# First batch: the coarse 1/sum moves from a GpSimd product into the matmul that transposes

## The chip, the cores and the metric

One core of a Trainium2 chip runs the whole program. The metric is the device time of one execution in microseconds (us). The kernel before takes 667.07 us, the median of three runs (666.96 to 668.61). A core has TensorE (PE, matmuls), VectorE (DVE), ScalarE (ACT), GpSimd (POOL) and SyncE (SP, which issues the loads and stores here), each with its own instruction list that it works through in order.

## The reference, cut to what matters

Three layers in a row, on 4 batches of 576 positions. The first is an attention of 8 heads of 64, the sum of two parts:

```python
q_d = q.reshape(B, H, Sd, 4, D).mean(axis=3)       # k_d, v_d likewise: 144 positions
out_d = sm_attn(q_d, k_d, v_d)                     # softmax(q k^T / 8) v, coarse
out_up = np.repeat(out_d, 4, axis=2)
mask = np.abs(pos[:, None] - pos[None, :]) < 4     # local: 7 neighbours
out = out_up + softmax(masked scores) @ v
```

The second adds the real part of a Fourier transform over positions and features, normalises, and applies two weight matrices of 512x2048 and 2048x512 with a ReLU between them. The third is a gated convolution with two weights of 512x512. Of all this the change touches the softmax of the coarse attention: exp(s) divided by its sum, times v.

## The kernel before, in words

**Stages.** The attention and the Fourier step of batch 0 are written out in `chain0`; those of batches 1 to 3 in `attn_steps`. The two later layers run in 12 units of 192 positions; the attention of a later batch is worked in between the units of an earlier one. Batch 0 has nothing to be worked in between, except the preparation of the weights: they come as 64-bit words, and three integer operations on VectorE (`word_op`, lines 547 and, through the helper `stt`, 448) rebuild each block of 128x1024 as 32-bit floats. The first layer's matmuls (line 1160, in f32 for the first positions, and 1196 with two halves in f16) need the centred result u (line 1711) of batch 0.

**The coarse attention of batch 0.** Four items a = 0 to 3, of two heads each (`par`). For each item: `coarse` puts the scores of 144x144 into PSUM as two halves of 72 rows (line 1518); `coarse_max` takes the row maxima on VectorE; `coarse_exp` makes exp on ScalarE into the tile E with the row sums beside it (line 1534); `coarse_norm` adds 1e-9 to the sums, takes the reciprocal (lines 1539, 1540) and multiplies E by it on GpSimd, one product of 72x288 per head (through the helper `mul`, so its line is 451):

```python
for par in range(2):
    mul(G, E[:, par], E[:, par], s_[:, par].unsqueeze(2).to_broadcast([QC, 2, SD]))
```

`coarse_turn` transposes E in four pieces of 72x72 per head on TensorE, with E as the stationary operand and the identity `eye` as the moving one (line 1549), and ScalarE evicts the result as ET (line 1552); `coarse_value` multiplies it by v (line 1558) into `base`.

**Beside it** runs the local attention of batch 0 in three groups: scores (line 1439), maxima, exp on ScalarE in pieces of 64 columns (line 1462), normalisation on VectorE (`score_norm`), transposes (line 1476), values (line 1495), and the sum with `base` into X on VectorE (`value_add`). The Fourier step follows.

**In batches 1 to 3** the coarse attention is in `lowres`; there the normalisation is either GpSimd's product (`if b in EN_G`, which holds batch 1 alone) or two ScalarE products of 72x144 per head (line 906).

**Order of the work.** Each step of the program has a number, in the order in which the steps are written into the program. The table `ORDER` gives for each engine its whole instruction list in these numbers ("48.1" is the second instruction of step 48 on that engine). Steps that the text names: 48, 54, 71, 85 are the normalisations of the items a = 0 to 3; 75, 68, 73 are three weight operations; 2, 4, 7, 9 the loads of the parts of q (7 and 9 the second parts, 9 for items 2 and 3), 1, 3, 6, 8 those of k; 11, 13, 14 those of v0, v1, v2; 16.1 a table of 512 KB for the Fourier step. `CHAIN0` gives the order in which batch 0's steps are written. Before the first loads arrive, TensorE runs filler matmuls on the tile `busy` (`fill`, line 1418), which GpSimd has set to 1.

Of the kernel before, what the change touches and what calls it, by code (L numbers as in the profile page):

```python
# [9 lines left out]
F32 = mybir.dt.float32  # L10
# [9 lines left out]
SD = S // 4  # L20
# [60 lines left out]
263.1 296.2 291.2 302 296.1 291.3 394.0 265.0 288.3 265.2 298.3 265.1 288.0 263.3 265.3 306 315 267.0-1 319 269.0-1  # L81
295.0 267.2 269.2 296.0 301 327 272.0 288.1 272.1 274.0 288.4 274.1 288.5 298.2 275.0 288.2 275.1 311 298.0-1 289.3
277.0-1 289.0 277.2 289.1 289.4-5 289.2 277.3 278 394.1 283.0-1 318.0-1 283.2 334 330 283.3-4 286.0 291.4 286.1-2
342.0 314 342.1 318.2 283.5 303.0 305.0 283.6 290.2 290.1 320.1 346 320.3 290.0 318.3 321.1 321.3 303.1 320.0 320.2
323.1 305.1 349 321.0 331 325.0 324 356 321.2 323.3 323.0 323.2 325.1 326.3 326.1-2 326.0 333 394.2 363 339.0 336.0
339.1-2 336.1 325.2-3 347.0 347.3 347.2 337.1 337.0 339.3 348.3 348.2 348.0 351.0 370 394.3 351.2 347.1 339.4 348.1
339.5-7 358 351.3 337.2-3 378 384 353.2-3 339.8-9 368.3 394.4 351.1 368.0 353.0-1 339.10 388 316 368.1 368.4 368.2
368.5 369.0 372.3 396 372.0 364.0 369.1 374.0 393.0 364.1 372.1-2 372.4-5 393.1 400.1 402.1 376.0 374.1 376.3 383.2-3
405 399 376.1 406.1 376.2 376.4-5 380.3 380.0 400.0 400.3 416 413 380.1 402.0 380.2 380.4-5 374.2-3 426 374.4 383.0
406.0 390.0 383.1 387.0-1 418 391.0 429 387.2 390.1 391.2 390.2 391.1 390.3 387.3 391.3 390.4 395.1 395.0 390.5-6  # L90
398.0-1 395.2 390.7 398.2 390.8 522.0 432 390.9 400.2 404 446.1 374.5 435 402.3 402.2 410.1 406.2-3 374.6 390.10 408
439 407 446.0 410.0 410.3 441 410.2 411.0 411.2 411.1 443 522.1 411.3 430.0 414 457 423.0 436.0-1 423.1 428.1 428.0
430.1 449 446.2 436.2-3 422 436.4 428.2 455 428.3 436.5 434.1 444.1 436.6 434.0 444.3 436.7 425 447.1 458 444.0 444.2
462 436.8 447.0 447.3 447.2 450.3 450.2 450.1 522.2 453.3 450.0 453.2 453.1 436.9-11 434.2-3 453.0 451.1 451.0 463.0
460.0 436.12-13 466 468 460.1 522.4 436.14 451.2-3 473 463.1 478 483.0 486.3 486.0 489 480 481.0 486.4 486.1 486.5
481.3 481.2 488.3 427 492.3 492.0 486.2 483.1-2 504 483.3 492.1 499 483.4 488.2 492.4 492.2 492.5 495.0 503 483.5-8
488.0 490.3 497.3 497.0 495.1 509 506.2 483.9 522.3 497.4-5 497.1-2 495.2 490.0 490.2 481.1 502.3 502.0 495.3 488.1
# [1833 lines left out]
```

## Time and profile before

| | |
|---|---|
| median of the runs | 667.07 us |
| profiled execution, its own time | 668.18 us |
| its span, first to last instruction | 666.4 us |
| TensorE busy | 647.4 us (97%) |
| VectorE busy | 458.3 us (69%) |
| ScalarE busy | 328.5 us (49%) |
| GpSimd busy | 127.1 us (19%) |
| mean granted clock of TensorE | 0.985 of 2.4 GHz |

The profile is that of one execution. The busy times are sums over stages that have different limits; which engine a stage waits for is read from its timeline and its waits. A granted clock of 0.50 is 1.2 GHz. In the rows, `out<-in` are the tiles written and read, `x8` counts records, and what stands in brackets is the idle time of that engine just before, with what ended it.

### The profile page before, as it was taken

What the parts mean: (1) busy time and instruction counts of PE and PEld (TensorE: products, weight loads), DVE (VectorE), ACT (ScalarE), POOL (GpSimd) and SP (SyncE); (2) the same over time, 40 slices, a digit from 0 to 9 for tenths busy, and PEclk for the clock granted to TensorE, in tenths of its full rate; (3) what the DMA queues carried; (4) which work ended last, traced back from release to release, by engine and by line L of the source; (5) the groups of instructions that cost most, each with busy time, mean ns of one, the idle gap of its engine ahead of it and who ended that gap; (6) DMA issues with size and microseconds to landing.
All of it is one profiled execution on the core that took longest, in us unless ns stands there. A gap on an engine that the chain in (4) does not pass through costs nothing.

```text
span 666.4 us, 18165 instructions
## 1 busy us (share of the span) xinstructions
PE 647.4 (97%) x7751; PEld 581.6 (87%) x7751; DVE 458.3 (69%) x950; ACT 328.5 (49%) x997; POOL 127.1 (19%) x178
## 2 busy tenths in 40 slices
PE   8968999999999999999999999999999999999997
PEld 4647799999998887989988898998999989999895
DVE  3679999989998877657876645675447763562344
ACT  3665577888334757675235576643232313312122
POOL 0240306321210613501110352030001020000000
PEclk9959999999999999999999999999999999999999
DMA  8976072313424001403240020000300000000001
GB/s 301 402 247 243 2 253 82 101 34 100 161 60 171 20 18 46 142 1 104 77 150 2 27 62 17 3 1 25 116 2 17 2 1 33 1 2 18 2 32 48
DMA packets 23299, 52.08 MB, mean 78 GB/s; under 512 B 1855, under 2 KB 11071, under 8 KB 22194
## 3 DMA queue, kind: packets, MB, share of 16 engines
q1 hardware_dynamic: 23218, 50.91, 22.4%
q8 instruction: 61, 1.00, 0.6%
q14 instruction: 20, 0.16, 0.1%
HBM read 44.41 MB, written 8.26 MB: 79 GB/s over the span
## 4 chain that ended last, share of the span: by engine, by line
PE 78%; DVE 11%; issue 5%; DMA 3%; POOL 2%; ACT 1%; SPq 0%; POOLq 0%; ACTq 0%
PE ph L1196 25%; PE pc L1216 24%; PE out L1324 7%; PE val L1308 7%; DVE W L448 5%; PE ab L996 2%; POOL E L451 1%; PE dO L805 1%; PE po L1572 1%; PE st L1080 1%; PE sc L883 1%; DMA raw<-in_moe_w_ch_dram 1%; PE pc L1171 1%; DMA kTa<-in_k_dram 1%; PE dPT L788 1%
## 5 line engine op out<-in xcount | busy, mean ns | idle before, releaser
L1196 PE MATMUL ph<-uh,W 128*128 128x192 f16 x1408 | 198.3, 246 | 1.3 <-DVE hl L448 0.7
L1196 PEld LDWEIGHTS <-W 128*128 128x128 f16 x2112 | 176.8, 98 | 9.5 <-issue 4.3
L1216 PE MATMUL pc<-hh,W 128*128 128x192 f16 x1232 | 171.7, 246 | 0.0
L1196 PE MATMUL ph<-ul,W 128*128 128x192 f16 x704 | 171.2, 246 | 0.0
L1216 PEld LDWEIGHTS <-W 128*128 128x128 f16 x1848 | 154.3, 98 | 5.7 <-issue 1.4
L1216 PE MATMUL pc<-hl,W 128*128 128x192 f16 x616 | 129.5, 246 | 0.0
L1200 ACT ACTIVATE hh<-ph 128x384 f16<-128x384 f32 x88 | 42.7, 488 | 125.8 <-PE ph L1196 100.5
L448 DVE SCALAR_TENSOR_TENSOR hl<-ph,hh 128x384 f16<-128x384 f32 x88 | 48.2, 552 | 77.6 <-ACT hh L1200 77.4
L448 DVE SCALAR_TENSOR_TENSOR W<-X,cw,W 128x192 f32<-128x192 f32 x160 | 64.1, 437 | 2.7 <-ACT W L1271 2.3
L1308 PE MATMUL val<-yy,W 128*128 128x192 f16 x576 | 59.6, 246 | 0.5 <-ACT yy L1250 0.5
L1308 PEld LDWEIGHTS <-W 128*128 128x128 f16 x576 | 48.5, 98 | 1.1 <-issue 0.4
L1324 PE MATMUL out<-W,gh 128*128 128x512 f16 x144 | 46.5, 379 | 0.0
L769 ACT ACTIVATE dP<-dS,dmx 128x64 f32<-128x64 f32 x120 | 36.2, 329 | 0.6 <-PE dPT L788 0.3
L448 DVE SCALAR_TENSOR_TENSOR W<-W,W 128x1024 int32<-128x1024 int32 x24 | 29.5, 1237 | 0.1
L451 POOL TENSOR_TENSOR E<-E,lsu 72x288 f32<-72x288 f32 x16 | 18.9, 1197 | 55.1 <-ACT nm L1529 19.7
L454 POOL TENSOR_TENSOR sq<-sq 128x384 f32<-128x384 f32 (+1 forms) x12 | 10.6, 880 | 93.6 <-ACT sq L1091 93.2
L1324 PE MATMUL out<-W,gl 128*128 128x512 f16 x72 | 27.1, 379 | 0.0
L769 ACT ACTIVATION_READ_ACCUMULATOR dP<-dS,dmx 128x1 f32 x120 | 26.7, 223 | 0.0
L1324 PEld LDWEIGHTS <-gh 128*128 128x128 f16 x144 | 14.0, 98 | 12.0 <-issue 0.2
L1216 PE MATMUL pc<-hh,Wz 128*128 128x192 f16 x176 | 24.3, 246 | 0.0
L1171 PE MATMUL pc<-h,W 128*128 128x192 f32 x128 | 23.3, 329 | 0.0
L1160 PE MATMUL ph<-u,W 128*128 128x192 f32 x128 | 22.5, 327 | 0.4 <-DVE u L1711 0.4
(288 smaller groups left out, 1212.0 us busy)
## 6 DMA issues: line engine op xcount, KB each, us to landing
W<-in_moe_w_ch_dram SPq DMA_DIRECT2D x12, 1024.0 KB
out_dram<-osb SPq DMA_DIRECT2D x17, 256.0 KB
vw<-in_vw_dram SPq DMA_DIRECT2D x8, 512.0 KB
v<-in_vp_dram SPq DMA_DIRECT2D x24, 144.0 KB
X<-in_q_dram SPq DMA_DIRECT2D x6, 576.0 KB
kT<-in_k_dram SPq DMA_DIRECT2D x4, 582.0 KB
X<-in_moe_w_ch_dram SPq DMA_DIRECT2D x2, 1024.0 KB
raw<-in_moe_w_ch_dram SPq DMA_DIRECT2D x4, 512.0 KB
```

What stands on the lines that cost most here:

```text
L448: return eng.scalar_tensor_tensor(out=out, in0=in0, scalar=scalar, in1=in1, op0=op0, op1=op1)
L451: return eng.tensor_tensor(out=out, in0=a, in1=b, op=ALU.mult)
L454: return eng.tensor_tensor(out=out, in0=a, in1=b, op=ALU.add)
L769: A.activation(out=s_[:, z, a], in_=pss[par][:, z, a], func=AF.Exp, scale=SCALE, bias=mx[:, par, z, a:a + 1], accum_out=su[:, par, z, a:a ...
L996: T.matmul(out=ps[0:n, c0:c1], lhsT=d[x][:, c, sd, e, n0:n0 + n], rhs=feat[:, w, c, c0:c1], start=(t == 0), stop=(t == 5),)
L1160: T.matmul(out=ps[:, e], lhsT=W[AT[kc * 2 + m // 8] + 1][:, o:o + 128], rhs=u()[:, kc, :], start=(kc == 0), stop=(kc == 3))
L1171: T.matmul(out=c["ps"][m // 2][:, m % 2], lhsT=W[9 + g][:, o:o + 128], rhs=hs[g // 2][:, g % 2, e, :], start=(kk == 0 and m % 2 == 0), sto ...
L1196: T.matmul(out=ps[:, e], lhsT=w1_ap(pw, kc, 2 * g + e), rhs=uh[px][:, kc, :], start=(t == 0), stop=(t == 11))
L1200: A.activation(out=h_, in_=ps, func=AF.Relu)
L1216: T.matmul(out=ps[m // 2][:, m % 2], lhsT=w2_ap(pw, kk, m), rhs=x[px][:, e, :], start=(kk == 0 and (pw, px) == (0, 0) and m % 2 == 0), sto ...
L1308: T.matmul(out=ps[:, e], lhsT=wv_ap(pw, kc, 2 * mh + e), rhs=m_["y"][px][:, kc, :], start=(t == 0), stop=(t == 11))
L1324: T.matmul(out=ps, lhsT=(gh, gl)[px][:, kc, t * 128:(t + 1) * 128], rhs=wo_ap(pw, kc), start=(n == 0), stop=(n == 11))
```

## The change

In batch 0, `coarse_norm` no longer multiplies E. VectorE makes, per head, a tile `dg` of 72 x (2 x 72) from the identity and the reciprocal sums: two diagonal matrices. `coarse_turn` then multiplies E by the diagonal matrix instead of the identity, as a plain f32 matmul in place of the transpose; the result is the transposed and scaled E. `EN_G` becomes empty, so batch 1 uses ScalarE's products like batches 2 and 3. The tile `busy` is 128 columns wide in place of 512, and the filler matmul reads it four times over. All five lists of `ORDER` are new, the tile slots are not.

```diff
-EN_G = (1,)
+EN_G = ()
...
-    busy = const.tile([P, 512], F16, name="busy")
+    busy = const.tile([P, P], F16, name="busy")
...
-                    T.matmul(out=ps, lhsT=busy[:, 0:P], rhs=busy, start=True, stop=True)
+                    T.matmul(out=ps.rearrange("p (a c) -> p a c", c=P), lhsT=busy, rhs=busy.unsqueeze(1).to_broadcast([P, 4, P]), start=True, stop=True)
...
             V.reciprocal(out=s_, in_=s_)
             for par in range(2):
-                mul(G, E[:, par], E[:, par], s_[:, par].unsqueeze(2).to_broadcast([QC, 2, SD]))
+                lr["dg", a, par] = sp.tile([QC, 2, QC], F32, tag="dg", name="dg", bufs=3)
+                mul(V, lr["dg", a, par], eye[0:QC, 0:QC].unsqueeze(1).to_broadcast([QC, 2, QC]),
+                    s_[:, par].unsqueeze(2).to_broadcast([QC, 2, QC]))
...
-                        T.transpose(out=pe[:, kc, qc], in_=lr["E", a][:, par, qc, kc * QC:(kc + 1) * QC],
-                                    identity=eye[0:QC, 0:QC])
+                        T.matmul(out=pe[:, kc, qc], lhsT=lr["E", a][:, par, qc, kc * QC:(kc + 1) * QC],
+                                 rhs=lr["dg", a, par][:, qc], start=True, stop=True)
```

Of the new lists, the starts that bear on batch 0 (SyncE's, GpSimd's and VectorE's):

```diff
-0 2 1 4 7 3 5.0 11 5.1 6 13 9 8 14 10 15.2 12 15.1 16.0 15.3-4 195.1 16.1 15.0 119.2 15.5 119.3 185.0 123.1 16.2 119.0
+0 2 1 4 3 5 13 11 6 16.0 7 14 16.1 8 9 10 15.0-1 12 15.3 15.5 15.4 119.2 185.0 15.2 195 123.1 123.0 122.0 16.2 119.0
...
-0.0 5 48.1 48.0 54 71 85 136.1 136.0 137 139.1 139.0 0.1 195.1 195.0 195.2 183.0-1 183.3 183.2 193 211.1 211.0 229
+0.0 5 136 195.1 0.1 137 139.1 139.0 121 195.0 183.0-2 193.0-6 183.3 193.7-8 211.1 211.0 286.0 229.1 195.2 217.0-1
...
-21 20 30 18 25 32.0-1 32.3 32.2 41 48.0 38.1 38.0 48.1 28 23 27 58.0 54 65 58.1 0 31 71 77.1 77.0 60 34 81.0 85.0 81.1
-85.1 42 55 59 67 68 75 83 52.0 86 52.1 81.2 131.0 52.2-3 81.3 93 81.4-5 92 70.0 129 70.1 56 70.2-3 97 63 98 73 102 79
+30.0 20.1 20.0 30.1 18 21 32 25 28 41 48.0 38 48.1 23 0 131.0 48.2-3 54.0 56 27 54.1 63 31 54.3 54.2 34 58.0 131.1 42
+65 59 58.1 55 71.0 131.2 71.1-3 77 75 68 73 85 81.0 84 81.1 86 67 81.2 52.0 81.3 52.1 130 52.2-3 70.0 92 70.1 93 70.3
```

## Rows read from the trace of the kernel before

**Rows 1.** The page's busy time, share of the span and instructions, of TensorE.
```profile
PE 647.4 (97%) x7751; PEld 581.6 (87%) x7751; DVE 458.3 (69%) x950; ACT 328.5 (49%) x997; POOL 127.1 (19%) x178
```

**Rows 2.** Stretches: length, then each engine's busy us, granted clock, DMA.
```profile
9.07:79.00 69.93, 59.00 (x707) 44.36 (x707) 57.68 (x112) 43.71 (x175) 17.94 (x21) 0.85 0.70 253
10.00:30.00 20.00, 18.91 (x267) 13.22 (x267) 13.73 (x29) 13.13 (x68) 2.58 (x4) 1.00 1.02 396
30.00:50.00 20.00, 13.94 (x141) 10.07 (x143) 14.92 (x34) 13.78 (x73) 10.24 (x4) 0.54 0.80 265
31.00:32.00 1.00, 0.82 (x6) 0.38 (x5) 1.00 (x3) 0.51 (x3) 1.00 (x2) 0.84 1.00 327
41.00:52.00 11.00, 10.31 (x126) 8.18 (x127) 7.24 (x20) 7.70 (x39) 0.72 (x2) 0.50 0.44 92
50.00:79.00 29.00, 26.15 (x310) 21.07 (x306) 28.11 (x50) 16.80 (x37) 5.12 (x13) 0.96 0.39 141
140.00:170.00 30.00, 30.00 (x413) 28.34 (x410) 27.84 (x70) 23.34 (x66) 5.78 (x8) 1.00 0.24 79
```

**Rows 3.** TensorE's waits to 130 us: total, times, longest.
```profile
PE eT L1549 <- POOL E L451: 4.5, 1, 4.5
...
PE po L1418 <- POOL busy L472: 1.3, 1, 1.3
```

**Rows 4.** GpSimd's timeline: start, us, line, operation, idle before.
```profile
21.12 1.29 POOL L451 TENSOR_TENSOR E<-E,lsu 72x288 f32<-72x288 f32 x2 [19.67 <-ACT nm L1529]
...
30.94 2.94 POOL L451 TENSOR_TENSOR E<-E,lsu 72x288 f32<-72x288 f32 x2 [2.28 <-DVE lsu L1540]
34.42 7.30 POOL L451 TENSOR_TENSOR E<-E,lsu 72x288 f32<-72x288 f32 x2 [0.54 <-DVE lsu L1540]
```

**Rows 5.** Tile lsu: minimum, median, maximum ns, of whole run.
```profile
L906 ACT ACTIVATE E<-E,lsu x32: 397/402/419, 280.5 to 431.4; 72x144 f32<-72x144 f32 x32
...
L451 POOL TENSOR_TENSOR E<-E,lsu x16: 661/665/6678, 21.1 to 169.6; 72x288 f32<-72x288 f32 x16
```

**Rows 6.** TensorE's timeline, two sets of transposes.
```profile
29.04 0.67 PE L1549 MATMUL eT<-eye,E 72*72 72x72 f32 x8 [0.70 <-ACT base L1560]
...
41.15 1.32 PE L1549 MATMUL eT<-eye,E 72*72 72x72 f32 x8 [4.50 <-POOL E L451]
```

**Rows 7.** ScalarE's timeline, the eviction behind the stall.
```profile
41.88 0.41 ACT L1552 ACTIVATE ET<-eT 72x288 f32<-72x288 f32 x1 [4.58 <-PE eT L1549]
```

**Rows 8.** VectorE's waits to 130 us: total, times, longest.
```profile
DVE dsu L1467 <- ACT dP L1462: 4.2, 1, 4.2
```

**Rows 9.** TensorE's timeline, the first matmuls of the first layer.
```profile
79.00 2.87 PE L1160 MATMUL ph<-u,W 128*128 128x192 f32 x16 [0.41 <-DVE u L1711]
```

**Rows 10.** VectorE by form, 14 to 47 us: busy us, mean ns.
```profile
L448 DVE SCALAR_TENSOR_TENSOR W<-X,W 128x1024 int32<-128x1024 int32 x4 | 4.8, 1200 | 0.0
...
L547 DVE TENSOR_SCALAR W<-W 128x1024 int32<-128x1024 int32 x4 | 2.7, 683 | 0.0
...
L451 DVE TENSOR_TENSOR dP<-dP,dsu 128x256 f32<-128x256 f32 x2 | 0.8, 422 | 0.0
...
L451 DVE TENSOR_TENSOR tr<-cv,eye 128x128 f32<-128x128 f32 x1 | 0.3, 291 | 2.6 <-PE cv L1585 2.6
```

**Rows 11.** TensorE by form, to 56 us: records, busy us, mean ns.
```profile
L1549 PE MATMUL eT<-eye,E 72*72 72x72 f32 x32 | 4.5, 277 | 5.2 <-POOL E L451 4.5 <-ACT base L1560 0.7
L1476 PE MATMUL dPT<-eye,dP 128*128 128x128 f32 x20 | 4.5, 386 | 0.4 <-DVE dP L451 0.4
L1518 PE MATMUL sc<-qkT 64*72 64x144 f32 x32 | 3.6, 295 | 0.3 <-ACT E L1534 0.3
```

**Rows 12.** TensorE's waits after 130 us, first and last of four.
```profile
PE ph L1196 <- DVE hl L448: 0.7, 1, 0.7
...
PE pq L1019 <- ACT DS L1046: 0.2, 1, 0.2
```

**Rows 13.** ScalarE's waits from 130 to 200 us.
```profile
ACT hh L1200 <- PE ph L1196: 8.1, 5, 2.7
```

More of the change, by code (lines that the diff above doesn't have):

```diff
@@ L81 @@
[L81 to L85, printed above, removed]
@@ new lines @@
+216.0-1 219 197.4 173.1-2 197.5 220 188 239.4-6 250 221 189 251 231.3 231.0 217.1 222 224 247.2 231.4 247.0-1 257
+241.3 247.3 217.0 231.1 241.0 231.2 231.5 225 245.0 216.2-3 226 216.4-5 245.1 228 284.0 241.1 245.2 261 266 241.2
+241.4 245.3-4 241.5 249.3 245.5 249.0 284.1-2 233 294.0 294.2-3 245.6-8 270 245.9 291.0 245.10 249.1 245.11 249.2
+295.3 295.2 245.12 296.2 245.13 235 253.0-1 245.14 249.4-5 255.3 255.0 284.3-4 259.1 280 295.0 255.4 276 255.1-2
+253.2-3 238 294.1 253.5 284.5 253.4 243 255.5 285.0 295.1 285.1-5 259.0 292 287.1 297 263.0 265.0 287.0 263.2 263.1
@@ L141 @@
+590.2 602 605 609 595 593.1 606 612 601 614 621 619 607 610 620.1-2 620.0 632 627 623.0 634 620.3 638 635 625 623.1
+641 643 649 631 636 651 648 656 639 660 650.3 650.2 650.1 650.0 663 666 664 654 668 670 683 685 677 661 686.1 674 675
+684 688 686.0 687 689 690 691
 """,
     "tensor": """
[L143 to L144 removed]
@@ new lines @@
+324.0-3 356.14-20 363.3-8 333.17-22 324.4-7 356.21-23 363.9-20 324.8-11 370.0-3 333.23 370.4-11 335.0-3 357.22
+357.16-17 357.23 370.12-18 363.21-23 335.6 335.4-5 335.8 335.7 335.9-19 366.6 366.0 366.7 366.1 366.8 366.2 366.9
+366.3 370.19-21 336 378.0-13 366.10-11 366.4-5 339.0 366.18-20 366.12 366.21 366.13-15 366.22-23 366.16 378.14-20
+370.22 341 337.0-31 337.33 337.32 339.1 378.21-23 366.17 373.6 373.0 370.23 373.1-3 373.7-8 373.4 345 388.0-1 373.9-10
+373.5 373.11-12 373.18 373.13 373.19-22 373.14-16 373.23 373.17 381.0 381.6 381.1 381.7-8 350.4-6 350.0 350.7 381.2
@@ new lines @@
+437.20-21 437.14 437.22 437.15 437.23 438.6 408.0-21 437.16-17 408.22-23 438.0-2 438.7-10 438.3 438.11 438.4-5
+438.12-13 438.18-20 438.14-16 438.21-22 438.17 438.23 423.22-23 443.0-9 441.0-13 443.10-11 411.9 411.0-1 411.10
+411.2-3 411.11-15 411.4 411.16-17 411.5-8 441.14-23 411.18-26 443.12-15 445.6 443.16-23 449.0-3 414.0-1 445.0-1 445.7
+445.2 445.8 445.3 445.9-10 445.4-5 445.11 414.2-5 414.9 414.6 414.10-12 414.7 414.13 414.8 414.14-17 449.4-18
+445.12-14 445.18 445.15 445.19-21 445.16 445.22 445.17 445.23 455.0-1 452.0 428.1 428.0 428.2-17 455.2-21 436.0 452.1
@@ new lines @@
+452.6-8 449.19 452.2-3 452.9-10 452.4 452.11 455.22-23 449.20-23 446.0-6 462.0-13 452.5 452.18 452.12-14 452.19
+452.15-16 452.20-23 452.17 434.0 462.14 446.7 456.0 456.6-9 456.1-3 456.10-11 456.18 456.4-5 458.0-8 462.15-17
+458.9-12 446.8-11 436.1 456.12 456.19 462.18-19 458.13-16 434.1 456.13 448.0-3 458.17-20 434.2-29 448.4-12 448.14
+448.13 448.15-19 434.30-31 434.33 434.32 462.20 456.14-16 456.20-23 456.17 458.21-23 459.0-8 462.21-23 461.0 461.6
+461.1 460.0-3 459.9-11 461.2-3 461.7 461.4-5 461.12-14 461.8-9 461.15 460.4-6 468.0 463.0-1 460.7-20 468.1-7 461.10-11
@@ new lines @@
+461.16 461.18 461.17 461.19-20 466.0-5 468.8-17 461.21 460.21-23 451.0-1 461.22 466.6-10 451.2-31 451.33 451.32
+464.0-1 466.11-16 468.18 461.23 466.17-23 468.19-23 464.2 464.6 464.3 464.7-8 464.4-5 464.9 464.12 464.10 464.13
+464.11 464.18-19 464.14-15 464.20-23 464.16-17 463.2-23 478.0-6 465.0-2 465.4-7 465.3 480.0 467.6-8 467.0 467.9
+467.1-3 467.10 467.4-5 467.12 467.11 467.18-20 467.13 467.21 467.14-16 467.22 467.17 467.23 465.8-9 465.12 465.10
+465.13 465.16 465.11 465.14 465.17 465.20-21 465.15 465.18-19 465.22-26 465.28 465.27 465.29-36 465.38-39 465.37 470.0
@@ new lines @@
+594.5 594.12 594.19 594.13 593.1 597.19 602.11-19 594.20-21 594.14 606.0 602.20-23 597.20-23 594.15 594.22 594.16-17
+594.23 599.0-1 599.6-8 599.2 599.9 599.3 599.10-11 599.4-5 599.12 599.18-19 599.13-16 599.20-22 599.17 599.23 595.0-2
+603.0-1 603.6 603.2-3 603.7 603.4-5 603.12 603.8-10 603.13-16 603.11 603.18-19 603.17 603.20-21 605.0-16 606.1
+605.17-23 603.22-23 609.0-4 595.3-11 612.0 609.5-8 606.2 609.9-23 612.1-13 606.3-5 608.6-7 608.0 608.8 612.14-21
+614.0-6 607.0 608.1-2 608.9 614.7-8 608.3 608.10 608.4 608.11 608.18 608.5 614.9-17 612.22-23 608.19-21 608.12-15
@@ new lines @@
+608.22 608.16-17 608.23 606.6-7 611.6 611.0 611.7 611.1 611.8-10 611.2-3 611.11 611.18 611.4-5 606.8-11 611.12-14
+611.19-21 611.15-16 611.22 611.17 611.23 607.1 610.0-1 613.0 613.6-8 613.1 613.9-10 613.2-4 613.11 613.5 613.12 613.18
+613.13 613.19-22 613.14 607.2-9 619.0-4 614.18-23 610.2-10 613.15-17 613.23 615.0 615.6 619.5-11 621.0-7 607.10-11
+619.12-14 607.12 610.11-12 621.8-23 619.15-16 615.1 615.7-8 615.2 615.9 615.3-4 619.17 610.13-14 619.18 615.5
+615.12-13 615.10-11 615.18-22 615.14-16 615.23 615.17 619.19 616.0 616.6 616.1 616.7 616.2-3 616.8-9 616.4 616.10
@@ L296 @@
+669.11 669.14-15 669.18-21 669.16-17 669.22-23 670.18-23 671.6-8 671.0-1 671.9-10 671.2-5 671.11-12 671.18-19
+671.13-16 671.20-21 671.17 671.22-23 672.0 672.12 672.1-11 672.13-23 675.0-17 685 675.18 674.4-23 688.0-7 689.0-9
+688.8-19 675.19-23 688.20-23 689.10-23 687 690.0-5 691.0-3 690.6-11 691.4-11
 """,
```

416 lines of the change are left out of this document (195 added, 221 removed), and 7 rows, old and new, of the table ORDER.

## The prediction

> **What bounds the kernel now.** I began with the page's busy shares: TensorE is busy 97% of the 666.4 us span [rows 1], so a change can win only where TensorE stands or where its clock is low. The stretches of the span say where that is [rows 2]: from 140 to 170 us TensorE has no gap at all, at full clock, while from 30 to 50 us it is busy 13.94 of 20 us at a granted clock of 0.54. This is the first batch's attention, which nothing else can hide, since the first layer's large matmuls need its result. The list of TensorE's waits up to 130 us names one large one: 4.5 us for GpSimd's product at line 451, writing E [rows 3]. The timelines show what happens there. GpSimd does the 1/sum products in pairs; two pairs take 1.29 us, the third 2.94, and the last runs from 34.42 to 41.72, 7.30 us [rows 4]. Its longest single product takes 6,678 ns where the median is 665 [rows 5]. VectorE meanwhile runs the integer operations that rebuild the weights. TensorE stands 4.5 us until the transposes at 41.15 [rows 6]. ScalarE, in order, has the eviction of these transposes ahead of the exponentials of two local groups and stands 4.58 us; VectorE then stands 4.2 us, because its next instruction wants those exponentials [rows 7, 8]. So one late GpSimd result holds three engines for over four microseconds. After it VectorE is nearly full, 28.11 of the 29 us from 50 to 79 [rows 2], until the centred u and the first layer's first matmul at 79.00 [rows 9]. From there on TensorE's list is full, so the end should follow that instant nearly one for one.
>
> **The change part by part.** *Removed in the first batch:* eight GpSimd products (four pairs), 12.8 us of GpSimd time together [rows 4]. Only the last pair's excess is on the path. Its sums' reciprocal, the last instruction before it, was ready before 34.42.
>
> *Added on VectorE:* eight products of 72x144 that make the diagonals. None is in this trace. From below: 128x128 takes 0.291 us; from above: 128x256 takes 0.422 [rows 10]. The straight line between them gives 0.31 at 144 columns, which I take: 8 x 0.31 = 2.5 us (2.3 to 3.4). VectorE has idle time that can take it: from its first instruction at 9.07 us to 79 it is busy 57.68 of 69.93, so 12.2 us are idle, the 4.2 among them [rows 2, 8]. If none of this idle time served, the 2.5 us would all be late.
>
> *The new wait:* the last transposing matmul waits for VectorE in place of GpSimd. In VectorE's new list three weight operations (steps 75, 68, 73) stand between the last maxima and the last sums' step 85: 1.2 + 0.7 + 1.2 = 3.1 us [rows 10]. If the last sums are ready as before, at about 34.3, the two diagonals end between 34.3 + 0.6 = 34.9 and 38.0. Apart from the 4.2 us VectorE is idle only 0.9 of the 20 us there (14.92 busy, [rows 2]), so I take the late end, 38.0 against 41.72: 3.7 us earlier. Queued behind these diagonals on VectorE are the weight operations and the local normalisations, which need ScalarE's exponentials; TensorE's values step waits for those.
>
> *TensorE:* 32 transposes become 32 plain f32 matmuls. The trace has both kinds: the 16 matmuls of the coarse scores (line 1518, four for each of four items) leave 32 records, two each, while the 20 transposes of line 1476 and the 32 of line 1549 leave one each [rows 11]. A record of 72 columns is issued every (0.67 - 0.22)/7 = 0.064 us at full clock (eight records span 0.67 us, the last of them 0.22) [rows 6], so the change adds 32 x 0.064 = 2.0 us of TensorE time, and twice that at half clock. TensorE is not the limit before 36 us, so only the last item's eight are on the path: 0.5 us, or 1.0 at the half clock that stands there. I take 1.0 off the 3.7.
>
> The Trainium skill bears on this term: "TensorE: Matmul & The Clock Gate", Terms (the entry on the streaming buses), says that the transpose mode is four times faster for FP32. By it the eight last matmuls would cost three extra records each, 1.5 us at full and 3.1 at half clock, 2.1 more than I take. The trace disagrees: an f32 matmul leaves two records, not four, and a pass of an f32 matmul is issued at the pace per column of a transpose, (2.87 - 0.33)/15 = 0.169 us for 192 columns [rows 9].
>
> *After the stall:* VectorE is the nearer limit. Its idle falls by the 4.2 us; of the other 8.0 us I expect a third, 2.7, to be used, as the new list puts weight operations where it waited; it gains 2.5 us of work. That is 4.2 + 2.7 - 2.5 = 4.4 us; the bounds are 4.2 - 3.4 = 0.8 and 12.2 - 2.3 = 9.9. The path through the last diagonal gives 3.7 - 1.0 = 2.7. The two meet at the local normalisations; I take their mean, 3.5 us.
>
> *Loads:* in SyncE's new list the second parts of q and k for items 2 and 3 come behind the 512 KB of v2 and the 512 KB table, those for items 0 and 1 behind v0 and v1. At the 396 GB/s of 10 to 30 us [rows 2] a megabyte is 2.6 us. The cover is VectorE's and TensorE's other work, since these parts are wanted only at about 16 us; I charge nothing, and up to 2.6 us if the cover fails.
>
> *The second batch:* eight GpSimd products (0.665 us median, [rows 5]) become 16 ScalarE products of 402 ns, as batches three and four have them [rows 5]: 6.4 us on ScalarE between 140 and 170 us. ScalarE is busy 23.34 of these 30 us [rows 2], so 6.7 are free. I charge 0, with 0 to 6.4 as bounds.
>
> *The smaller edits:* the busy tile's memset shrinks from 0.53 us and the filler matmuls read it by a repeated pattern. TensorE's first filler waits 1.3 us for the memset [rows 3], but these fillers only pass the time until the first k and q are loaded, so nothing. The searched orders elsewhere have little to win: TensorE's four waits for other engines after 130 us, of 0.7 to 0.2 us, total 2.0 [rows 12]. Bounds -2 to +2 us; I take 0.
>
> **Sum.** The profiled execution took 668.18 us with a span of 666.4, 1.8 of it around the span. 668.18 - 3.5 = 664.7 for such an execution; it lies 1.1 above the median of the runs, 667.07, so I predict 667.07 - 3.5 = 663.6.
>
> **The rivals.**
> *A, the clock comes back too:* TensorE's 11 us from 41 to 52 run at 0.50 (1.2 GHz) [rows 2], and four idle microseconds lie before. Without them the clock may be at full for the values and transposes that follow, some 10 us of work that would take 5. VectorE's own list, bounded by 9.9, caps it. For it: the standstill goes, and 32 more records fill gaps. Against: the clock fell between 31 and 32 us (0.84) already, before the long wait [rows 2]. About 3.5 us more: 660.1. The Trainium skill leans this way ("TensorE: Matmul & The Clock Gate", Part 4: PE-mode transpose, says that transposes do not count as TensorE work for the clock as matmuls do).
>
> *B, the wait only changes its owner:* the last diagonal is late in VectorE's list, because the start is later (2.6 us of loads) or the lists in front are longer. Then it ends at about 38.0 + 2.6 = 40.6 and the gain is 41.72 - 40.6 - 1.0 = 0.1. For it: VectorE is the fullest engine there. Against: 12.2 us of idle. 667.0.
>
> *C, slower: ScalarE in the second batch.* Between 140 and 170 us it has 6.7 us free and gets 6.4. If the products stand ahead of the first layer's evictions (line 1200), TensorE, which has no gap there, waits for each. It decides when ScalarE's busy share reaches 10 of 10 while TensorE's falls under 10; price up to 6.4 us, less the 3.5 won: 670.0. Against: ScalarE's waits there are mostly for TensorE (8.1 us for line 1196 up to 200 us, [rows 13]), so it has room.
>
> **How the numbers follow.** Forecast 0.55, A 0.18, B 0.17, C 0.10. A difference under 0.3% (2.0 us) can't be told from none here. Faster than 665.1 are A and nearly all of the forecast's own range (661.5 to 665.5): 0.70. Within: B and the rest: 0.20. Slower: C: 0.10. The range from 659 to 667.5 leaves out the far part of A and C, and holds the unknown costs: 3.4 for the diagonals, 2.6 for the loads.
>
> **What would show it.** Right: no GpSimd instruction between 20 and 42 us; eight VectorE products of 72x144 at 0.3 us; 64 records for the transposing matmuls; no TensorE wait above 2 us between 30 and 50; the first matmul of line 1160 at 75 to 76 us; everything behind it earlier by as much. A shows a clock of 1.00 by 45 us. B shows TensorE waiting for VectorE's diagonal at about 38 to 41. C shows TensorE gaps between 140 and 175 us that end with ScalarE. The forecast is wrong if the first layer starts earlier and the end doesn't: then VectorE's weight work, or a load, is the limit between 80 and 200 us.

## The result, and the profile after

The changed kernel takes 661.12 us (median; 660.89 to 661.76), beside 667.84 for the kernel before on the same chip: a ratio of 0.9897, 95% interval [0.9872, 0.9922]. A second measurement gave 661.51 beside 667.03, 0.9914 [0.9900, 0.9927]. So it gains 5.5 to 6.7 us, and 663.6 was 2.5 too high. The profiled execution took 661.18 us, its span is 659.4.

One instant cuts the gain in two: the first layer's first matmul, called F below. Before, F stands at 79.00 us [rows 9] with 587.4 us of span behind it. The timeline of TensorE after has it at 73.39, with 586.0 behind it: 5.6 us are won ahead of F and 1.4 behind it. These two are the difference of two profiled executions and add up to 7.0 us, more than the medians show, because the execution before was a long one (668.18 us, beside medians of 667.0 to 667.8). Behind F three other runs with the old lists have 586.8, so 0.8 us is the safer figure there.

```profile
73.39 2.54 PE L1171 MATMUL ph<-u,W 128*128 128x192 f32 x14 [0.57 <-DVE u L1724]
```

The stretches of the kernel after, with the columns of [rows 2] (length, then busy us of TensorE, weight loads, VectorE, ScalarE, GpSimd; clock; DMA share; GB/s):

```profile
9.07:79.00 69.93, 67.18 (x786) 52.65 (x778) 65.10 (x129) 45.89 (x177) 2.57 (x13) 0.90 0.72 252
30.00:50.00 20.00, 18.19 (x232) 14.51 (x232) 19.45 (x42) 14.07 (x71) 0.00 (x0) 0.66 1.04 308
41.00:52.00 11.00, 10.22 (x187) 8.42 (x187) 10.66 (x23) 4.53 (x19) 0.00 (x0) 0.73 1.04 267
140.00:170.00 30.00, 30.00 (x413) 28.18 (x412) 27.68 (x69) 23.39 (x70) 1.21 (x1) 1.00 0.16 55
```

Read the third busy column first. VectorE is idle 69.93 - 65.10 = 4.8 us up to 79 us, where it was idle 12.2 [rows 2]; none of the 4.8 lie behind F. From 30 to 50 us it is now the fullest engine, 19.45 of 20. Its list begins with another instruction, 1.6 us later than before (the kernel before, then the kernel after):

```profile
9.07 1.35 DVE L1510 TENSOR_REDUCE qkT<-X 128x288 f32<-128x1152 f32 x1 [9.07 <-DMA X<-in_q_dram]
10.67 1.95 DVE L1463 TENSOR_REDUCE dmx<-dS 128x8 f32<-128x512 f32 x4 [10.67 <-PE dS L1450]
```

From this first instruction to F VectorE takes 62.7 us, where it took 69.9. Its wait for the exponentials, 4.2 us before [rows 8], is down to 0.4, and that for the coarse scores from 2.4 to 0.7 (the first line is the kernel before):

```profile
DVE nm L1525 <- PE sc L1518: 2.4, 3, 1.2
...
DVE nm L1536 <- PE sc L1529: 0.7, 1, 0.7
DVE dsu L1478 <- ACT dP L1473: 0.4, 1, 0.4
```

TensorE's waits up to 130 us (total, times, longest), the largest two and the one for a diagonal:

```profile
PE po L1571 <- ACT ET L1565: 1.0, 3, 0.6
PE po L1429 <- POOL mirror L492: 1.0, 1, 1.0
...
PE eT L1562 <- DVE dg L462: 0.2, 1, 0.2
```

The 4.5 us for GpSimd [rows 3] are gone and no wait of that size has come in their place. The last item's steps in VectorE's timeline, then in TensorE's:

```profile
34.40 1.21 DVE L459 SCALAR_TENSOR_TENSOR W<-X,W 128x1024 int32<-128x1024 int32 x1
35.53 0.68 DVE L558 TENSOR_SCALAR W<-W 128x1024 int32<-128x1024 int32 x1
36.13 1.22 DVE L459 SCALAR_TENSOR_TENSOR W<-W,W 128x1024 int32<-128x1024 int32 x1
37.46 0.17 DVE L1550 TENSOR_SCALAR lsu<-lsu 72x4 f32<-72x4 f32 x1
37.66 0.17 DVE L1551 RECIPROCAL lsu<-lsu 72x4 f32<-72x4 f32 x1
37.87 0.52 DVE L462 TENSOR_TENSOR dg<-eye,lsu 72x144 f32<-72x144 f32 x2
```
```profile
38.32 2.17 PE L1562 MATMUL eT<-dg,E 72*72 72x72 f32 x16 [0.18 <-DVE dg L462]
40.42 0.74 PE L1571 MATMUL po<-ET,vr 72*64 72x144 f32 x2
```

The diagonals end at 38.39, behind the three weight operations, where GpSimd's pair ended at 41.72 [rows 4]. The last item's values begin at 40.42; before, they began 2.0 us later:

```profile
42.40 1.85 PE L1558 MATMUL po<-ET,vr 72*64 72x144 f32 x8
```

The operations by form, TensorE's up to 56 us, VectorE's from 14 to 47 (count, busy us, mean ns, idle before):

```profile
L1562 PE MATMUL eT<-dg,E 72*72 72x72 f32 x64 | 7.2, 281 | 0.2 <-DVE dg L462 0.2
```
```profile
L462 DVE TENSOR_TENSOR dg<-eye,lsu 72x144 f32<-72x144 f32 x8 | 2.1, 298 | 0.1
L462 DVE TENSOR_TENSOR dP<-dP,dsu 128x256 f32<-128x256 f32 x2 | 0.8, 422 | 0.0
L462 DVE TENSOR_TENSOR tr<-cv,eye 128x128 f32<-128x128 f32 x1 | 0.3, 280 | 0.0
```

32 records have become 64, and 4.5 us of busy time 7.2 [rows 11]. A pair of diagonals takes 0.52 us, so the eight cost 2.05. The last line tells of the new order: `tr` had 2.6 us of idle before it [rows 10] and has none now.

### The profile page after: what moved, and what is told of

Read it like the earlier page. It is cut to its first block, busy times and chain, and to the rows that moved or that the text cites. A ratio compares the mean times of both kernels' runs of the same rounds, so it can differ in the third digit from the quotient of the medians.

```text
span 659.4 us, 18222 instructions
## 1 busy us (share of the span) xinstructions
PE 650.5 (99%) x7783; PEld 585.1 (89%) x7783; DVE 447.1 (68%) x958; ACT 332.6 (50%) x1013; POOL 100.6 (15%) x162
## 4 chain that ended last, share of the span: by engine, by line
PE 66%; DVE 0%; ACT 0%; POOL 0%; issue 0%; ACTq 0%
PE ph L1207 22%; PE pc L1227 22%; PE out L1335 7%; PE val L1319 7%; PE ab L1007 1%; PE st L1091 1%; PE dO L816 1%; PE po L939 1%; PE sc L894 1%; PE pp L1030 1%; PE pq L1030 1%; PE dPT L799 1%; PE eT L929 1%; PE dS L766 1%; PE pn L1030 0%; PE tps L1292 0%
## 5 line engine op out<-in xcount | busy, mean ns | idle before, releaser
L1207 PE MATMUL ph<-uh,W 128*128 128x192 f16 x1408 | 203.0, 246 | 0.5 <-ACT uh L1135 0.5
L1227 PE MATMUL pc<-hh,W 128*128 128x192 f16 x1232 | 174.6, 246 | 0.0
L459 DVE SCALAR_TENSOR_TENSOR W<-X,cw,W 128x192 f32<-128x192 f32 x160 | 61.3, 418 | 5.2 <-ACT W L1282 4.8
L1319 PE MATMUL val<-yy,W 128*128 128x192 f16 x576 | 61.0, 246 | 0.0
L1227 PEld LDWEIGHTS <-Wz 128*128 128x128 f16 x264 | 22.2, 98 | 1.7 <-DVE X L465 1.2
```

The lines of the kernel that those rows point to most:

```text
L459: return eng.scalar_tensor_tensor(out=out, in0=in0, scalar=scalar, in1=in1, op0=op0, op1=op1)
L1207: T.matmul(out=ps[:, e], lhsT=w1_ap(pw, kc, 2 * g + e), rhs=uh[px][:, kc, :], start=(t == 0), stop=(t == 11))
L1227: T.matmul(out=ps[m // 2][:, m % 2], lhsT=w2_ap(pw, kk, m), rhs=x[px][:, e, :], start=(kk == 0 and (pw, px) == (0, 0) and m % 2 == 0), sto ...
L1319: T.matmul(out=ps[:, e], lhsT=wv_ap(pw, kc, 2 * mh + e), rhs=m_["y"][px][:, kc, :], start=(t == 0), stop=(t == 11))
```

## The experiments

Every ratio is to the kernel before on the same chip.

| run | median us | ratio, 95% interval | VectorE starts, us | F, us | span, us | span less F |
|---|---|---|---|---|---|---|
| before | 667.0 to 667.8 | 1 | 9.07 | 79.00 | 666.4 | 587.4 |
| after | 661.12 | 0.9897 [0.9872, 0.9922] | 10.67 | 73.39 | 659.4 | 586.0 |
| after, again | 661.51 | 0.9914 [0.9900, 0.9927] | 10.15 | 73.00 | 659.0 | 586.0 |
| 1 old lists, diagonals | 663.90 | 0.9953 [0.9939, 0.9967] | 8.51 | 75.35 | 662.1 | 586.8 |
| 2 new lists, GpSimd products | 662.38 | 0.9937 [0.9924, 0.9950] | 10.04 | 74.58 | 660.6 | 586.0 |
| 3 old, weight words later | 668.81 | 1.0031 [1.0019, 1.0042] | 7.85 | 79.38 | 666.2 | 586.8 |
| 4 batch 1 on GpSimd, one block | 664.16 | 0.9960 [0.9947, 0.9972] | 10.33 | 73.04 | 662.4 | 589.4 |
| 5 old start of the loads | 671.46 | 1.0056 [1.0043, 1.0069] | 10.96 | 83.68 | 669.9 | 586.2 |
| 6 transposes kept | 660.70 | 0.9893 [0.9880, 0.9906] | 10.74 | 72.95 | 658.9 | 586.0 |
| 7 old, TensorE kept busy | 668.66 | 1.0017 [1.0007, 1.0026] | 8.24 | 78.77 | 665.6 | 586.8 |
| 8 diagonals made twice | 663.45 | 0.9938 [0.9926, 0.9951] | 10.95 | 75.79 | 661.8 | 586.0 |
| 9 batch 1 on GpSimd, spread | 663.93 | 0.9950 [0.9937, 0.9962] | 10.80 | 73.58 | 662.1 | 588.5 |
| 10 diagonals by ScalarE | 664.66 | 0.9961 [0.9948, 0.9974] | 10.38 | 78.01 | 664.0 | 586.0 |
| 11 old order of q and k alone | 661.25 | 0.9912 [0.9898, 0.9925] | 10.66 | 72.97 | 659.3 | 586.3 |

F moves by a few tenths from one profile to the next without any edit (73.39 and 73.00 for the same kernel), so F alone tells nothing under half a microsecond. Most of that is the start: from VectorE's first instruction to F the two take 62.72 and 62.85 us. Within one set of lists this difference is the better measure; the old lists start earlier because they begin with another instruction. Starts, F and span are those of one profiled execution, which is not always near the median: that of run 10 is the slowest of five (665.75 us), those of runs 3 and 7 are the fastest of six (667.98) and of eleven (667.42).

**1. The diagonals alone.** The kernel before, with its own lists; the eight GpSimd products become diagonals at the place of VectorE's reciprocals, and the fillers are as in the change.

```diff
-0.0 5 48.1 48.0 54 71 85 136.1 136.0 ...     (GpSimd's list)
+0.0 5 136.1 136.0 ...
-... 85.1 42 55 59 67 68 75 83 ...         (VectorE's list)
+... 85.1-3 42 55 59 67 68 75 83 ...
```

> The kernel before with its own lists and batch 1 as it was; only the diagonal (VectorE's two products stand right behind the reciprocal of each item) and the narrower busy tile. Theory (the late GpSimd product is the loss): TensorE's wait of 4.5 us at the last transposes goes, the first matmul of the first layer comes 4 to 6 us before 79.0, time 662 to 664. Rival (the new lists bring the gain): within 1 us of the kernel before, since VectorE only takes over a wait.

F comes 3.65 us earlier (3.1 from VectorE's start), somewhat less than the theory's 4 to 6, and the time falls by 3.1 us. The largest waits of TensorE up to 130 us, which say what is late next:

```profile
PE mir L1639 <- DVE X L454: 2.1, 2, 1.5
PE dPT L1476 <- DVE dP L451: 1.1, 1, 1.1
```

The stall at GpSimd is gone, and the two largest waits are now for VectorE; the first was there before (1.8 us), the second was 0.4.

**2. All but the diagonals.** The kernel after (new lists, batch 1 on ScalarE, the narrower tile), with batch 0's products put back on GpSimd and plain transposes.

```diff
+0.0 5 48 54 71 85 136 195.1 ...           (GpSimd's list)
-mul(V, lr["dg", a, par], eye ..., s_ ...)
+mul(G, E[:, par], E[:, par], s_ ...)
```

> The changed kernel with its new lists, but batch 0's products back on GpSimd and plain transposes. Theory: the last products again run beside VectorE's weight operations and take 3 us or more in place of 0.67, TensorE waits for them, time 664 to 667. Rival (new lists): 661 to 662, as the new lists put the work right whoever multiplies.

4.2 us of the gain stay without any diagonal (4.6 by the medians); the time lies between the two ranges. The diagonals are still worth something: TensorE waits 2.7 us in all for GpSimd's products, the longest 1.2, and from VectorE's first instruction to F it takes 64.5 us in place of 62.7 to 62.9. GpSimd's timeline shows why so much stays; its columns are those of [rows 4]:

```profile
21.58 1.29 POOL L462 TENSOR_TENSOR E<-E,lsu 72x288 f32<-72x288 f32 x2 [20.46 <-ACT nm L1540]
24.78 4.24 POOL L462 TENSOR_TENSOR E<-E,lsu 72x288 f32<-72x288 f32 x2 [1.92 <-DVE lsu L1551]
33.36 1.28 POOL L462 TENSOR_TENSOR E<-E,lsu 72x288 f32<-72x288 f32 x2 [4.34 <-ACT base L1571]
37.98 1.73 POOL L462 TENSOR_TENSOR E<-E,lsu 72x288 f32<-72x288 f32 x2 [3.34 <-ACT base L1571]
```

The long pair has moved: here it is the second, which takes 4.24 us, and the last takes 1.73 instead of 7.30. In the old list two-input operations on the weights run from 35.35 to 40.57 us, inside the pair's time; in the new one they begin at 40.19, when it is done. VectorE pays as well: its one-input operations beside the last pair are 1.02 and 1.09 us long where they take 0.68 elsewhere:

```profile
38.17 1.02 DVE L558 TENSOR_SCALAR W<-W 128x1024 int32<-128x1024 int32 x1
...
39.18 1.09 DVE L558 TENSOR_SCALAR W<-W 128x1024 int32<-128x1024 int32 x1
```

**3. The late product without its cause.** The kernel before, with seven weight operations moved behind the normalisations of the local groups.

```diff
-85.1 42 55 59 67 68 75 83 52.0 86 52.1 81.2 131.0 52.2-3 81.3
+85.1 52.0 52.1 81.2 52.2-3 42 55 59 67 68 75 83 86 131.0 81.3
```

> The kernel before with seven weight operations of VectorE moved behind the local normalisation, so that none runs beside the last pair of GpSimd products. Theory (these operations hold GpSimd up): the pair takes 1.3 us in place of 7.3 and TensorE's wait of 4.5 us shrinks below 1; the time changes little, -3 to +1 us, because VectorE then idles instead. Rival (the product is slow by itself): the pair still takes 7 us.

GpSimd's last pair shrinks from 7.30 us [rows 4] to the 1.29 of an undisturbed one, with nothing changed but what VectorE does beside it:

```profile
33.05 1.29 POOL L451 TENSOR_TENSOR E<-E,lsu 72x288 f32<-72x288 f32 x2 [0.40 <-ACT ET L1552]
```

The time does not fall; it rises by 1.8 us, beyond the range that the theory gave. VectorE now stands 5.70 us for ScalarE's exponentials with its weight words undone, and TensorE waits for VectorE in GpSimd's place:

```profile
PE dO L1495 <- DVE dsu L1467: 6.4, 1, 6.4
```

So the late product by itself is not what the gain is worth. What VectorE does in that time counts, as run 8 shows below.

**4 and 9. Batch 1's products back on GpSimd.** The kernel after with `EN_G = (1,)` and without the 16 ScalarE products; in run 4 the four steps stand in one block in GpSimd's list, in run 9 with 259.1 ahead of the last.

```diff
-EN_G = ()
+EN_G = (1,)
-... 217.2-3 230 259.1 259.0 ...                    (GpSimd's list)
+... 217.2-3 230 231 241 249 255 259.1 259.0 ...    (run 4)
+... 217.2-3 230 231 241 249 259.1 255 259.0 ...    (run 9)
```

> The changed kernel with batch 1's eight products back on GpSimd (its ScalarE products gone, the lists otherwise the same). Theory (batch 1's part is worth nothing): 660.6 to 661.7. Rival (the 1.4 us that the change wins behind 79 us come from it): 662 to 663. Other rival (ScalarE was too full): 659 to 660.5.

> The changed kernel with the second batch's eight products back on GpSimd (their 16 ScalarE operations gone), now spread over GpSimd's list between its other work instead of all in one block ahead of it. Theory 'place in the list': the 3 us that the block cost were X<-X,base on GpSimd at 168.3 in place of 159.0 us; with 259.1 ahead of the last product that comes back, 661 to 662 us, and span less first matmul 586 to 587. Theory 'products': GpSimd's products there are late beside VectorE, whatever their place: 663.5 to 664.5, span less first matmul 589, and TensorE waits again for hl, AL and X behind 130 us.

Both lose 2.4 to 3 us against the kernel after (run 4 lies above all three of its ranges, run 9 in that of "products"), F stays where it was, and the loss stands behind F. In run 9 the product X<-X,base of GpSimd is back at 160.45 us (158.95 after, 168.27 in run 4), and the loss stays: the place in the list had a share of under 1 us. VectorE's groups by form from 130 to 175 us tell where the rest goes, run 9 first and then the kernel after:

```profile
L459 DVE SCALAR_TENSOR_TENSOR W<-W,s_w,W 128x1024 f16<-128x1024 f32 x7 | 9.6, 1371 | 0.0
...
L459 DVE SCALAR_TENSOR_TENSOR tap<-X,cw,tap 128x192 f32<-128x192 f32 x9 | 4.2, 499 | 0.0
...
L558 DVE TENSOR_SCALAR W<-raw 128x512 int32<-128x512 int32 x4 | 2.9, 726 | 0.0
```
```profile
L459 DVE SCALAR_TENSOR_TENSOR W<-W,s_w,W 128x1024 f16<-128x1024 f32 x7 | 8.8, 1264 | 0.0
...
L459 DVE SCALAR_TENSOR_TENSOR tap<-X,cw,tap 128x192 f32<-128x192 f32 x9 | 3.4, 410 | 0.0
...
L558 DVE TENSOR_SCALAR W<-raw 128x512 int32<-128x512 int32 x4 | 1.7, 434 | 0.0
```

In these three groups, the ones that differ most, the same instructions cost VectorE 16.7 us instead of 13.9 with GpSimd's products beside them. TensorE then has two waits behind 130 us that the kernel after does not have:

```profile
PE pq L1030 <- DVE AL L459: 1.0, 1, 1.0
...
PE ph L1207 <- DVE hl L459: 0.9, 1, 0.9
```

Together they are 1.9 us, most of the 2.5. With the old lists, the same products stood in batch 1 and span less F was 586.8 to 587.4; so 2.5 us is their price in lists searched for a kernel without them, and 0.8 to 1.4 us is what the move and the new lists gain together.

**5 and 11. The loads.** The kernel after with the whole old start of SyncE's list, and with the old order of q and k alone, the tables of step 16 staying ahead of the weights.

```diff
-0 2 1 4 3 5 13 11 6 16.0 7 14 16.1 8 9 10 15.0-1 12 ...
+0 2 1 4 7 3 5.0 11 5.1 6 13 9 8 14 10 16.0 15.0-1 12 16.1 ...        (run 5)
+0 2 1 4 7 3 5.0 11 5.1 6 13 9 8 16.0 14 16.1 10 15.0-1 12 ...        (run 11)
```

> The changed kernel with SyncE's first 17 loads in the order of before (the second parts of q and k ahead of v0, v1, v2 and the table). Theory (the loads are covered): 660 to 662, like the changed kernel, with VectorE's first instruction earlier and the rest the same. Rival (the new load order costs up to 2.6 us): 658 to 659.5. Other rival (the new load order is a part of the gain): 662.5 to 664.

> The changed kernel with the old order of the q, k and v loads at the start, but with the small table and feat kept ahead of the weights (feat issued at about 9.4 us, not at 12.6 as in the run with the whole old start). Theory 'feat's place': ScalarE's list wants feat at 20 us, right behind item 0's exponentials, and the whole loss came from that; now 661 to 662.5, first matmul at 73.3 to 75. Rival 'order of q and k': second parts of q and k ahead of the values' loads cost time by themselves: 665 or more, first matmul behind 77.

Run 5 loses 10 us, more than any of its theories allowed; run 11 loses nothing. ScalarE's waits of run 5 name the cause: the table `feat` is issued behind the first weights (12.58 us, not 9.01), and ScalarE's new list has its operation on feat right behind item 0's exponentials.

```profile
ACT neg L1626 <- DMA feat<-in_c_feat_dram: 6.2, 1, 6.2
```

VectorE and TensorE then stand for ScalarE 5.5 and 4.2 us, and the granted clock is at half from 28 to past 55 us. One load behind its turn cost more than the whole change gains; the order of q and k, which I had priced at up to 2.6 us, costs nothing.

**6. The second pass.** The kernel after with transposes, against an identity that VectorE makes with as many instructions as the diagonals, by a comparison in place of the product; batch 0's coarse part lacks its 1/sum.

```diff
-T.matmul(out=pe[:, kc, qc], lhsT=E[...], rhs=dg[:, qc], start=True, stop=True)
+T.transpose(out=pe[:, kc, qc], in_=E[...], identity=dg[:, qc])
```

> The changed kernel with true transposes again, against a tile that VectorE makes as before but by a comparison, so that it is the identity (the 1/sum of batch 0's coarse part is left out): the wait for VectorE stays, TensorE's second pass goes. Theory (two records in place of one, on the path only in the last item at half clock): 16 records fewer per pair of heads, first matmul of the first layer 0.5 to 1.1 us earlier, 659.5 to 660.7. Rival (four times a transpose): 3 us or more. Rival (hidden): within 0.3 us of the changed kernel.

32 records come back to 4.3 us busy in place of 64 with 7.2, and the time is 0.4 to 0.8 us lower than that of the kernel after by the medians, 0.3 to 1.4 by the ratios, with intervals that overlap. From VectorE's first instruction to F it takes 62.2 us in place of 62.7 to 62.9. So the second pass costs TensorE 2.9 us and the kernel about half a microsecond, if anything; four times a transpose, with its 3 us, is out.

**7. The clock alone.** The kernel before with 36 filler matmuls ahead of the last transposes, where TensorE stood idle.

```diff
+for _ in range(36 if (a, par) == (3, 0) else 0):
+    T.matmul(out=pe..., lhsT=busy[:, 0:QC], rhs=busy[:, 0:4 * QC], ...)
```

> The kernel before with 36 filler matmuls of 288 columns on TensorE ahead of the last item's transposes, where it waits for GpSimd; nothing else. The wait for GpSimd stays, the clock can come back before it ends. Theory (the half clock costs time by itself): the stretch from the last coarse values to the first mirror matmul, 12.5 us before, shortens by 1.5 to 4 us, time 663.5 to 666. Rival (VectorE's list is the limit there): the stretch shortens by under 0.5 us and the time stays within 0.7 us of the kernel before.

The fillers fill the gap and the clock rises (stretches, columns as above):

```profile
38.00:42.00 4.00, 3.96 (x35) 3.45 (x33) 1.63 (x2) 0.26 (x1) 2.77 (x2) 0.96 1.05 349
42.00:46.00 4.00, 2.42 (x40) 1.57 (x40) 1.47 (x6) 4.00 (x28) 0.00 (x0) 0.90 0.45 122
46.00:50.00 4.00, 3.66 (x68) 3.11 (x69) 4.00 (x12) 3.28 (x12) 0.00 (x0) 0.50 0.01 2
```

At 0.90 in place of 0.50 TensorE is busy only 2.42 of the 4 us from 42 to 46, where ScalarE is busy all 4; from 46 on VectorE is. From the last coarse values to the Fourier step's first matmul it takes 54.67 - 42.20 = 12.5 us, as before (54.89 - 42.40). Four microseconds of fuller clock win nothing there. The test has two limits. The clock is at half again from 46 us on, and the fillers run a little too long: they hold the last transposes until 41.29, 0.5 us after the end of GpSimd's pair (40.77), where they began 0.6 us ahead of it before (41.15 and 41.72, [rows 4, 6]).

```profile
35.47 5.99 PE L1548 MATMUL eT<-busy 128*72 128x288 f16 x36
41.29 0.67 PE L1551 MATMUL eT<-eye,E 72*72 72x72 f32 x8
```

VectorE waits 4.9 us for the exponentials in place of 4.2, and the median is 1.3 us above the kernel before, outside the 0.7 that the rival gave.

**8. Twice the diagonals.** The kernel after, each diagonal made twice.

```diff
-131.0 48.2-3 54.0 ... 31 54.3 54.2 34 ... 71.0 131.2 71.1-3 77
+131.0 48.2-5 54.0 ... 31 54.2-5 34 ... 71.0 131.2 71.1-5 77
```

> The changed kernel with each of the eight diagonals made twice on VectorE: 2.1 us more of VectorE's time in the first 38 us, nothing else. Theory (VectorE's list is the limit of this stage): the first matmul of the first layer and the end come 1.5 to 2.3 us later. Rival (VectorE has room, the path runs through TensorE and ScalarE): under 0.7 us later.

VectorE is busy 61.64 us up to F in place of 59.49, 2.15 more. F moves by 2.4 to 2.8 us and the median by 1.9 to 2.3 (1.6 to 2.7 by the ratios); from VectorE's first instruction to F it takes 64.84 us in place of 62.72, 2.12 more. What VectorE gets more, the kernel pays in full.

**10. The diagonals on ScalarE.** The kernel after; ScalarE copies the identity with 1/sum as its scale, four pieces per item, each in its list where the reciprocal should be ready.

```diff
-mul(V, lr["dg", a, par], eye ..., s_ ...)
+for qc in range(2):
+    A.activation(out=lr["dg", a, par][:, qc], in_=eye[0:QC, 0:QC], func=AF.Copy, scale=s_[:, par, qc:qc + 1])
```

> The changed kernel with the first batch's diagonals made by ScalarE (16 copies of 72x72 with a scale per partition) and no longer by VectorE. Theory 'VectorE's list is the bound up to the first layer, and TensorE close behind': VectorE loses 8 x 0.26 = 2.05 us, so the first matmul comes up to 2.0 us earlier, at 71.5 to 72.5, and the time is 659 to 660.3. Rival 'ScalarE is as full as VectorE': it is busy 10.54 of the 12 us from 30 to 42 and gets 16 x 0.21 = 3.4 us more, 8 of them between 30 and 42; its exponentials and evictions come later, TensorE and VectorE wait for them, first matmul at 74 to 76, 661.5 to 664.

It was to beat both kernels and gives more than half of the gain back. Two rows show how: the wait that is new in TensorE's timeline, and the stretches behind it.

```profile
26.66 0.74 PE L1563 MATMUL eT<-dg,E 72*72 72x72 f32 x8 [0.56 <-ACT vr L1590]
```
```profile
26.00:28.00 2.00, 1.44 (x15) 0.96 (x13) 1.97 (x3) 1.47 (x7) 0.00 (x0) 1.00 1.03 426
28.00:38.00 10.00, 10.00 (x62) 7.81 (x62) 5.83 (x15) 7.57 (x39) 0.00 (x0) 0.50 1.02 399
38.00:50.00 12.00, 10.58 (x90) 8.28 (x89) 10.26 (x23) 9.89 (x54) 0.00 (x0) 0.50 0.99 265
```

Four copies hold ScalarE for 1.09 us, its next evictions begin at 24.38 and 26.01 in place of 23.69 and 25.33, TensorE has a gap at 26 us, and its clock is at half from 28 to 52 us (from 33 to 47 in the kernel after). From 28 to 38 us TensorE is full at half clock and VectorE is idle for 4.2 us. So the rival "ScalarE" held, by its order and not by its fullness (8.84 of the 10 us from 20 to 30), and in this execution the low clock came on top, which neither theory had; F at 78.0 is later than both gave. The five executions give a rough division. The profiled one has a mean granted clock of 0.981 over its span; two others have 0.989 and 0.990, like the kernel after (0.989 to 0.992), and take 663.7 and 663.4 us, inside the rival's range. So about 2 us go with the order alone, and up to 2 more with the longer half clock; no trace of the two others is kept, so this rests on their mean clock.

**The kernel after, once more**, beside runs 9 to 11:

> The changed kernel itself, so that the three others have it beside them on the same chip. Both theories: 661.1 us (660.7 to 661.8), ratio 0.990, first matmul of the first layer at 73.4 us.

661.51 us, F at 73.00, both as given.

## Why the prediction was right, and where its size was off

The time lies in the range of 659 to 667.5 us, but that range is wide: the forecast gain was 3.5 us and the measured one 5.5 to 6.7.

*The late GpSimd result holds three engines.* Right. The wait is gone in the kernel after, and in run 1 with the lists otherwise as they were. What runs 2 and 3 add is that it was not GpSimd that was slow: the same pair takes 1.29 us where VectorE has no weight operation beside it. The Trainium skill has a rule for this ("SBUF — State Buffer", Who interferes with whom): a VectorE instruction with two inputs in SBUF and a GpSimd instruction that reads SBUF exclude each other. Rows 4, run 3 and run 9 agree that the two lengthen each other, with 7.30 against 1.29 us on the one side and 16.7 against 13.9 on the other. Two-input instructions are not all of it: one-input operations got longer too (1.02 and 1.09 us against 0.68 in run 2).

*The new wait for VectorE's diagonal.* Right: I took 38.0, and it ends at 38.39 behind the three weight operations.

*TensorE's 1.0 off the path.* Not settled, though the 64 records came as forecast. Run 6 takes the second pass out and wins 0.3 to 1.4 us by the ratios, about 0.5 from VectorE's start to F; that is likelier half of my 1.0 than all of it, but none and all are both within what can be told apart.

*After the stall.* This is the term that failed in its size. I had two answers, 4.4 us by VectorE's idle time and 2.7 by the path through the last diagonal, and took their mean, 3.5. Run 8 shows that VectorE's list sets F nearly one for one, so its idle time is the account: it fell from 12.2 to 4.8 us. The 4.2 for the exponentials fell by 3.8, the 2.6 ahead of `tr` went [rows 8, 10], the wait for the coarse scores fell by 1.7 and small ones by 0.9; the later first instruction took 1.6 back. Less 59.49 - 57.68 = 1.8 of added work, the 2.05 for the diagonals in the main, that is 5.6 at F. (F is VectorE's start plus its busy and its idle time, so the sum must come out; that it means something rests on run 8.) The term 4.4 was near. The path through the last diagonal did not bind: the last item's values came 2.0 us earlier and F 5.6. Taking the mean with it was wrong.

*Orders elsewhere, and batch 1, at nothing.* Also too small: behind F 0.8 to 1.4 us were won, from 586.8 (runs 1, 3 and 7) or 587.4 (the kernel before) to 586.0. I had bounded batch 1 by 0 and 6.4 us of loss and allowed no gain, because I looked at ScalarE's room only. Runs 4 and 9 show the other side, VectorE's operations, which GpSimd's products lengthen. How much of it is batch 1 and how much the lists isn't separated.

*Loads at nothing.* Right for q and k (run 11). That `feat` would matter I didn't see.

*Lists and diagonals together.* Alone the diagonals give 3.1 us and all the rest 4.2 (run 2, which has batch 1 on ScalarE as well); both give 5.5 to 6.7, somewhat less than the sum of 7.3. Either alone already takes away VectorE's stall of 4.2 us: it is gone in run 1 and 0.4 in run 2.

*The rivals.* A (the clock) gave 660.1, nearer to the time than mine, but not by its mechanism. At 45 us the clock is still at 0.50; it comes back at 47 rather than 52 us. In run 7 a fuller clock wins nothing from 42 to 46 us. In run 11 the clock is at half from 35 to 45 us, not from 33 to 47 as in the kernel after, and this wins 0.4 to 0.5 us from VectorE's first instruction to F (62.31) and 0.3 us of the time on the same chip, no more than the noise. The stretch from 30 to 42 us in run 11, then in the second profile of the kernel after:

```profile
30.00:42.00 12.00, 9.70 (x72) 7.27 (x70) 11.84 (x29) 10.60 (x62) 0.00 (x0) 0.71 1.03 358
30.00:42.00 12.00, 10.57 (x67) 8.14 (x66) 11.46 (x28) 10.23 (x58) 0.00 (x0) 0.60 1.03 361
```

In run 10 a longer half clock goes with a loss. So the clock hardly limits here, but it can; no run holds it at full all the way to F. The rule of the Trainium skill that I set beside A ("TensorE: Matmul & The Clock Gate", Part 4: PE-mode transpose) finds no support, though the test is weak, since the 32 pieces are a small part of TensorE's work: with transposes (run 6) and with matmuls the clock falls between 32 and 34 us and stays at half to 46. B (the wait changes owner): not in this kernel, where the wait for the diagonal is 0.2 us; in run 3 TensorE does come to wait for VectorE, 6.4 us, but for the local sums. C (ScalarE in batch 1): TensorE is busy 30.00 of the 30 us from 140 to 170, so no.

## What to carry to other kernels

Where one in-order engine is nearly full up to the instant that sets the end, count its idle time and the work that you add to it; here that sum was the better forecast, and a path through another engine was no second opinion to average with. Before pricing a move off GpSimd, look at what VectorE does at the same moment, since each lengthens the other. And lists that were searched together come and go together: one load out of its turn cost 10 us.

## What the hardware showed that I had not expected

- One and the same GpSimd product of 72x288 takes 0.66 us alone and up to 6.68 beside VectorE's weight operations [rows 5]. The cost goes both ways: a one-input VectorE operation of 128x1024 takes 1.02 to 1.09 us beside such a product, and 0.68 without.
- Short gaps went ahead of a long time at 1.2 GHz: 0.70 us before the transposes at 29.04 [rows 6], and half clock from 31 to 32 us on [rows 2]; 0.56 us at 26 us in run 10, and half clock from 28 to 52, though TensorE was busy all of the 10 us from 28 to 38. A gap alone does not decide it: in the kernel before TensorE stood 1.58 us with the granted clock at 1.00 before and after.

```profile
58.20 0.72 PE L1637 MATMUL mir<-X,mirror 128*128 128x289 f32 x2 [1.58 <-DVE X L454]
```

- An f32 matmul with a diagonal in place of the identity leaves two records where the transpose leaves one (7.2 and 4.3 us busy for the same pieces), and the kernel's time hardly tells the two apart (661.1 to 661.5 and 660.7).
